# A shorter filter-band set-up, a new order of the first loads, and a later first down projection in a convolution and gated feed-forward kernel

## The chip, the cores and the metric

The kernel runs on one core of a Trainium2 chip. The metric is the device time of one execution in microseconds (us), as the median of several runs. The span in a trace, from the first to the last instruction, is about 1.8 us shorter than that time.

## The reference

```python
# x: (8, 4096, 192); weight: (8 heads, 7 taps); gate, val: (192, 1536); out: (1536, 192)
w = softmax(weight, axis=-1)
x_pad = zeros of 6 rows ahead of each sequence, then x
conv[b, s, h, :] = sum over k of w[h, k] * x_pad[b, s + k, h, :]      # 24 columns per head
y = conv.reshape(32768, 192)
g, v = y @ w_gate, y @ w_val
out = (g * sigmoid(g) * v) @ w_out
```

A causal seven-tap filter, with one set of taps per head, is followed by a gated feed-forward layer over 32,768 tokens.

## The kernel before

The convolution is a matmul with a banded matrix built from the taps, named `wide`. It is built on the chip at the start: small matmuls spread the taps over the partitions (`tapbank`), a multiplication with a unit matrix makes `spread`, and four matmuls with 0/1 matrices `shift` put the taps in their places (`taps`); two engines then copy the result out of PSUM into `wide`.

Tokens go through in 64 blocks of 512. A block has 12 steps. One step (`gate_val`) projects to 128 of the 1536 hidden columns, with six half-row matmuls that run as three pairs; ScalarE then takes the activation and VectorE the product. The down projection (`acc`) is done in four slots per block, between steps. The first four blocks have a convolution of their own (`early`), with a transpose on TensorE (`eturn`), so that the first step can start soon.

```python
    xe_load(0)                    # rows of x for block 0, three DMAs
    load_w(0, 384)                # gate and val columns, three DMAs each call
    load_w(384, 1024)
    xe_tile(1)
    xe_load(1)                    # rows of block 1
    load_w(1024, Dff)
    load_wo(0, 6)
    load_wo(6, NCH)
    # ... cut ...
    def make_wide():
        # ... cut ...
        for i in range(2):
            for n in range(2):
                matmul(banks[n], shift[:, n, i], spread[:, i],       # 512 columns
                       start=(i == 0), stop=(i == 1))
        # ... cut: two casts on ScalarE, two on VectorE into wide
    # ... cut ...
    keep_warm(7)                  # 128x512 matmuls on zeros
    spread_taps()
    keep_warm(2)
    make_wide()
    early(0, ...)
    eturn(0, ...)
    for n in range(n_steps):
        # ... cut: early(1) is the work of n == 4, early(2) of n == 10, early(3) of n == 19
        gate_val(n)
        if j % 3 == 1:
            after = silu[n - 2] if n >= 2 else None
            # j 7 and 10: slots 1 and 2 of this block; j 1 and 4: slots 3 and 4 of the last one
        # ... cut: eturn(1) after step 6, eturn(2) after step 17
```

## Time and profile before

| what | value | read from |
|---|---|---|
| time | 793.54 us, three runs of 792.71 to 794.03 | the times |
| TensorE busy | 784.0 of 792.0 us | the page |
| block 0's convolution starts | 7.57 us | timeline of TensorE |
| step 0 starts | 9.97 us | timeline of TensorE |
| step 20 starts | 34.17 us | timeline of TensorE |

Lines of the page of the kernel before: the span, the busy time of TensorE with its share and instruction count, and the granted clock in tenths over 40 slices.

```profile
span 792.0 us, 28590 instructions
...
PE 784.0 (99%) x12018; PEld 493.9 (62%) x12018; DVE 584.1 (74%) x933; ACT 522.2 (66%) x910; POOL 67.4 (9%) x93
...
PEclk9999999999999999999999999999999999999999
```

TensorE has no free time to speak of, so only the start and the end of the program can shrink. The next lines are the timeline of TensorE in the kernel before. The columns are start, length, engine, line, operation, output and inputs, the shapes and the count; an idle time before and its releaser stand in brackets.

```profile
1.20 3.17 PE L643 MATMUL warm<-fill 128*128 128x512 f16 x7 [1.20 <-DVE fill L91]
4.30 0.36 PE L286 MATMUL tapbank<-eye,split 8*32 8x8 f16 x16
4.59 1.03 PE L643 MATMUL warm<-fill 128*128 128x512 f16 x2
5.43 1.58 PE L326 MATMUL taps<-spread,shift 128*128 128x512 f16 x4
7.57 0.83 PE L380 MATMUL cv<-xe,wide 64*64 64x72 f16 x64 [0.56 <-ACT wide L338]
8.89 1.14 PE L438 MATMUL turn<-ident,tme 128*128 128x128 f16 x15 [0.50 <-ACT tme L398]
9.97 0.39 PE L545 MATMUL gate<-xc,w 64*128 64x512 f16 x1
...
13.72 0.22 PE L380 MATMUL cv<-xe,wide 64*64 64x72 f16 x1
14.50 0.72 PE L380 MATMUL cv<-xe,wide 64*64 64x48 f16 x63 [0.56 <-DMA xe<-in_x_dram]
...
30.45 0.72 PE L438 MATMUL turn<-ident,tme 128*128 128x128 f16 x10 [0.34 <-DVE o_sb L627]
```

From 5.43 to 7.57 us the chain runs through the four band matmuls and the casts. Block 1's convolution starts at 13.72 us and stops after one matmul until its rows of x land. At 30.45 us block 2's transposes wait for VectorE to take the finished output out of PSUM. Next, what the weight loads of TensorE waited for between 9 and 24 us in the kernel before: who waited, for what, the total in us, how often, the longest.

```profile
PEld L380 <- DMA xe<-in_x_dram: 0.7, 1, 0.7
...
PEld L545 <- DMA w<-in_moe_w_val_dram: 0.5, 2, 0.3
```

These are the rows of block 1 and the weights of step 3. The table by windows of the same kernel gives for each stretch the busy time of the five engines, then the clock, the mean busy share of the DMA engines, and GB/s.

```profile
4.00:6.00 2.00, 2.00 (x21) 0.84 (x21) 1.70 (x7) 0.74 (x2) 2.00 (x5) 1.00 1.25 134
6.00:8.00 2.00, 1.44 (x41) 0.60 (x42) 0.95 (x3) 0.65 (x2) 2.00 (x4) 1.00 0.99 127
```

From 4 us on the DMA engines are full. A caution about the clock column: it reads 1.00 here, while the 512-column matmuls before 7 us stand 0.43 us apart and those after 10 us stand 0.215 us apart. There is no clock record before the first grant, and the view takes full speed for granted there. The spacing of the matmuls shows the true rate.

### The profile page before, as it was taken

How to read it: one execution, taken by the hardware profiler on the slowest of the kernel's cores; microseconds unless marked ns; L12 is line 12 of the kernel's file. 1: busy time of each engine (PE TensorE's matmuls, PEld its weight loads, DVE VectorE, ACT ScalarE, POOL GpSimd, SP SyncE). 2: the span in 40 equal slices, each digit the busy share in tenths (PEclk: the TensorE clock that was granted, in tenths of full speed). 3: DMA queues.
4: the chain of work that ended last, by engine and by line, in shares of the span. 5: the costliest groups of instructions: out<-in, count | busy, mean ns of one | idle time of the engine just before them, and what ended most of it. 6: DMA issues, size and time to landing. Idle time of an engine off the chain costs nothing.

```text
span 792.0 us, 28590 instructions
## 1 busy us (share of the span) xinstructions
PE 784.0 (99%) x12018; PEld 493.9 (62%) x12018; DVE 584.1 (74%) x933; ACT 522.2 (66%) x910; POOL 67.4 (9%) x93
## 2 busy tenths in 40 slices
PE   8999999999999999999999999999999999999997
PEld 4666666666666666666666666666666666666665
DVE  7677777777777867767777777777777777777775
ACT  5676766666666666757666666666667667676664
POOL 8111010010100101001010000100001010000000
PEclk9999999999999999999999999999999999999999
DMA  9999577786857778567894769858587794726311
GB/s 131 149 204 146 125 116 118 164 124 146 105 120 152 129 147 119 120 126 125 155 140 113 117 112 165 128 133 118 112 154 121 150 115 118 136 81 116 80 42 42
DMA packets 214961, 99.23 MB, mean 125 GB/s; under 512 B 148776, under 2 KB 213936, under 8 KB 213936
## 3 DMA queue, kind: packets, MB, share of 16 engines
q1 hardware_dynamic: 167424, 78.75, 49.3%
q0 software_dynamic: 47136, 18.45, 21.7%
q8 instruction: 94, 1.54, 0.8%
q14 instruction: 35, 0.29, 0.1%
q10 hardware_dynamic: 272, 0.20, 0.1%
HBM read 36.90 MB, written 41.16 MB: 99 GB/s over the span
## 4 chain that ended last, share of the span: by engine, by line
PE 97%; DMA 1%; POOL 1%; DVE 0%; ACT 0%; issue 0%; POOLq 0%
PE gate L545 61%; PE acc L571 32%; PE cv L469 2%; PE val L545 1%; DMA xe<-in_x_dram 1%; POOL w L162 0%; POOL xe L97 0%; PE acc L592 0%; PE cv L380 0%; PE turn L438 0%; DVE h L556 0%; ACT sig L554 0%; DVE o_sb L627 0%; DVE tm L486 0%; ACT o_sb L731 0%
## 5 line engine op out<-in xcount | busy, mean ns | idle before, releaser
L556 DVE TENSOR_TENSOR h<-sig,val 128x512 f16<-128x512 f16 x768 | 507.7, 687 | 195.4 <-PE val L545 192.9
L554 ACT ACTIVATE sig<-gate 128x512 f16<-128x512 f32 x768 | 458.5, 597 | 234.9 <-PE val L545 207.4
L545 PE MATMUL val<-xc,w 64*128 64x512 f16 x2304 | 539.1, 376 | 0.2 <-DVE tm L486 0.2
L545 PE MATMUL gate<-xc,w 64*128 64x512 f16 x2304 | 539.2, 376 | 0.0
L545 PEld LDWEIGHTS <-w 64*128 64x128 f16 x4608 | 221.0, 94 | 212.7 <-issue 1.2
L571 PEld LDWEIGHTS <-h 64*128 64x128 f16 x6096 | 257.8, 94 | 66.0 <-issue 6.1
L571 PE MATMUL acc<-wo,h 64*128 64x192 f16 x6096 | 298.8, 243 | 0.0
L97 POOL DMA_DIRECT2D x<-in_x_dram x40 | 31.6, 792 | 437.0 <-ACT sig L554 429.9
L486 ACT CAST tm<-cv 128x480 f16<-128x480 f32 x60 | 30.6, 562 | 22.1 <-PE cv L469 22.1
L486 DVE CAST tm<-cv 128x480 f16<-128x480 f32 x60 | 36.6, 652 | 2.6
L627 DVE COPY o_sb<-acc 128x384 f32<-128x384 f32 x63 | 34.7, 550 | 0.0
L497 POOL COPY tm<-tm 128x1280 f16<-128x1280 f16 x15 | 18.8, 1252 | 137.3 <-DVE tm L486 129.1
L626 ACT COPY o_sb<-acc 128x384 f32<-128x384 f32 x63 | 30.1, 478 | 0.0
L469 PE MATMUL cv<-x,band 64*32 64x240 f16 x960 | 18.2, 265 | 0.0
L469 PEld LDWEIGHTS <-band 64*32 64x32 f16 x960 | 10.1, 91 | 4.9 <-issue 4.7
L132 POOL MEMSET x<- 6x192 f16 x7 | 1.7, 248 | 59.7 <-PE cv L469 59.6
L97 POOL DMA_DIRECT2D xe<-in_x_dram x9 | 6.0, 692 | 0.4 <-issue 0.3
L643 PE MATMUL warm<-fill 128*128 128x512 f16 x9 | 4.2, 628 | 1.2 <-DVE fill L91 1.2
L398 ACT CAST tme<-cv 128x288 f16<-128x288 f32 x8 | 2.9, 401 | 2.5 <-PE cv L380 2.5
L380 PE MATMUL cv<-xe,wide 64*64 64x48 f16 (+1 forms) x256 | 3.2, 192 | 1.1 <-ACT wide L338 0.6
L380 PEld LDWEIGHTS <-wide 64*64 64x64 f16 x256 | 2.7, 108 | 2.5 <-ACT wide L338 1.1
L438 PE MATMUL turn<-ident,tme 128*128 128x128 f16 x45 | 3.3, 220 | 0.8 <-ACT tme L398 0.5
(53 smaller groups left out, 40.0 us busy)
## 6 DMA issues: line engine op xcount, KB each, us to landing
out_dram<-o_sb SPq DMA_DIRECT2D x63, 384.0 KB
scr<-tm SPq DMA_DIRECT2D x105, 130.0 KB
x<-x SPq DMA_DIRECT2D x28, 480.0 KB
x<-in_x_dram POOLq DMA_DIRECT2D x24, 480.0 KB, 9.4
x<-in_x_dram POOLq DMA_DIRECT2D x7, 468.0 KB, 7.4
xc<-scr SPq DMA_TRANSPOSE x180
scr<-tm SPq DMA_DIRECT2D x15, 104.0 KB
wo<-in_moe_w_out_dram POOLq DMA_DIRECT2D x2, 288.0 KB, 6.3
```

The costliest lines, as they stand in the source:

```text
L97: nc.gpsimd.dma_start(out=t[p0 + i0 : p0 + i1, w0 - at : w1 - at, :], in_=bass.AP(tensor=x_flat.tensor, offset=(t0 + size * w0 - pad + i0) ...
L380: nc.tensor.matmul(o[Q * c : Q * c + Q, at : at + w], wide[Q * r : Q * r + Q, a, h, :], xe[e][Q * r : Q * r + Q, c : 2 * G : 2, h * grp : ...
L469: nc.tensor.matmul(banks[r][32 * c : 32 * c + 32, t * w : t * w + w], band[Q * r : Q * r + Q, h, :], x16[u][Q * r : Q * r + Q, NG * c : NG ...
L486: eng(tm[u][:, NG * r : NG * r + NG, 2 * grp * hp : 2 * grp * hp + 2 * grp].rearrange("p g (t e) -> p g t e", t=2), banks[r][:, 0 : 2 * w] ...
L497: seq(nc.gpsimd.tensor_copy(tm[u][:, :, SL * Q : 4 * Q], tm[u][:, :, 0:Q]))
L545: nc.tensor.matmul(o, w16[p0 : p0 + Q, k, ts(j, P)], xc[b][k][p0 : p0 + Q, 0:TB], start=(k == 0), stop=(k == SL - 1),)
L554: silu[n] = seq(nc.scalar.activation(sg, g, AF.Silu)).ins
L556: seq(nc.vector.tensor_tensor(hj, sg, v, op=ALU.mult))
L571: nc.tensor.matmul(acc[b][bank][:, s, :], hj[p0 : p0 + Q, ts(2 * bank + s, P)], wo16[p0 : p0 + Q, j, :], start=(not second and j == 0 and ...
L626: seq(nc.scalar.copy(o_sb[:, 0:2, :], acc[b][0]))
L627: seq(nc.vector.tensor_copy(o_sb[:, 2:4, :], acc[b][1]))
L643: nc.tensor.matmul(warm, fill[:, 0:P], fill, start=True, stop=True, skip_group_check=True,)
```

## The change

The intent is to start step 0 about a microsecond sooner and to close the holes that follow. The change has four parts. The band comes from one product of 256 columns and four half-size matmuls. The rows of x that make the first window are loaded behind the bulk. An index that is needed later is made apart, ahead of the weight loads. In block 0, the second convolution moves behind step 5 and the down projection starts at step 9.

```diff
             if e == 0 and r == 0:
-                windows(xe[e], 0, 0, EO, 0, 1, i0=pad)
                 windows(xe[e], 0, 0, EO, 1, w1)
+                windows(xe[e], 0, 0, EO, 0, 1, i0=pad, i1=Q - 2)
...
-    jid = small("jid", [P, P], i32)
-    seq(nc.gpsimd.iota(jid, pattern=[[1, P]], base=0, channel_multiplier=0))
+    jn = small("jn", [P, 4, Q], i32)
+    seq(nc.gpsimd.iota(jn, pattern=[[-16, 4], [1, Q]], base=0, channel_multiplier=0))
     xe_tile(0)
-    seq(nc.vector.memset(xe[0][0:pad, 0, :], 0.0))
+    seq(nc.vector.memset(xe[0][0:Q, 0, :], 0.0))
     xe_load(0)
+    cid = small("cid", [P, P], i32)
+    seq(nc.gpsimd.iota(cid, pattern=[[1, P]], base=0, channel_multiplier=0))
     load_w(0, 384)
...                                     # (split is widened to 16 copies of each tap)
-        for i in range(2):             # 16 tap matmuls of 8x32
-            for a in range(2):
-                for d in range(4):
+        for a in range(2):             # 2 tap matmuls of 8x128
...
-        for i in range(2):
-            for n in range(2):         # 512 columns, in pairs that accumulate
-                    nc.tensor.matmul(banks[n], shift[:, n, i], spread[:, i],
-                        start=(i == 0), stop=(i == 1))
+        for n in range(4):             # 256 columns, each its own half of a bank
+                nc.tensor.matmul(banks[n // 2][:, c0 : c0 + 256], shift[:, n], spread,
+                    start=(n % 2 == 0), stop=True)
...
     keep_warm(7)
     spread_taps()
-    keep_warm(2)
+    keep_warm(5, P)                    # five of 128 columns
     make_wide()
...
-        if n == 4:                     # work of slot 4: early(1)
-        elif n in (10, 19):            # work: early(2), early(3)
+        if n in (11, 19):              # work: early(2), early(3)
...
         gate_val(n)
+        if n == 5:
+            early(1, (*acc_banks, gate_bank))
+        elif n == 7:
+            eturn(1, (*acc_banks, gate_bank))
+        elif n in (9, 11):
+            slot(1 if n == 9 else 2, b, silu[n - 1], work)
+        elif n == 13:
+            slot(3, 0, silu[n - 1])
+        elif j % 3 == 1 and b:         # as before
...
+        if n == 18:                    # was 17
             eturn(2, (*acc_banks, gate_bank))
```

More of the change, by code (lines that the diff above doesn't have):

```diff
@@ L202 @@
             load_x(1, r, low=low)
-    pm_i = small("pm_i", [P, 1], i32)
-    seq(nc.vector.tensor_single_scalar(pm_i, pid, 31, op=ALU.bitwise_and))
-    pm = small("pm", [P, 1])
-    seq(nc.vector.tensor_copy(pm, pm_i))
-    jf = small("jf", [P, P])
-    seq(nc.vector.tensor_copy(jf, jid))
-    p32 = small("p32", [P, 1])
-    seq(nc.vector.tensor_tensor(p32, pid, pm, op=ALU.subtract))
-    pd = small("pd", [P, 1])
-    eye = small("eye", [P, 32], fp16)
+    pq_i = small("pq_i", [P, 1], i32)
+    seq(nc.vector.tensor_single_scalar(pq_i, pid, 15, op=ALU.bitwise_and))
@@ L214 @@
+    pq = small("pq", [P, 1])
+    seq(nc.vector.tensor_copy(pq, pq_i))
+    pk = small("pk", [P, 1])
+    seq(nc.vector.tensor_tensor(pk, pid, pq, op=ALU.subtract))
+    eye = small("eye", [P, 16], fp16)
     seq(
         nc.vector.tensor_scalar(
-            eye, jf[:, 0:32], scalar1=pm, scalar2=None, op0=ALU.is_equal
+            eye, jn[:, 0, 0:16], scalar1=pq, scalar2=None, op0=ALU.is_equal
         )
     )
-    seq(
-        nc.vector.tensor_scalar(pd, p32, scalar1=1.0 / 32, scalar2=None, op0=ALU.mult)
-    )
@@ L222 @@
-    both = small("both", [P, 1])
-    seq(nc.vector.tensor_tensor(both, pm, pd, op=ALU.add))
-    eyes = small("eyes", [P, 32, 2, H], fp16)
-    seq(
-        nc.scalar.copy(
-            eyes.rearrange("p j a h -> p j (a h)"),
-            eye.unsqueeze(2).to_broadcast([P, 32, 2 * H]),
-        )
-    )
-    shift = small("shift", [P, 2, 2, 2, Q], fp16)
-    def make_shift(n, i):
-        seq(
-            nc.vector.tensor_scalar(
-                shift[:, n, i],
-                jf[:, 0:Q].unsqueeze(1).to_broadcast([P, 2, Q]),
-                scalar1=both, scalar2=32.0 * n + 4.0 * i,
-                op0=ALU.subtract, op1=ALU.is_equal,
-            )
-        )
@@ L243 @@
-    wexp = small("wexp", [H, K + 1])
-    seq(nc.vector.memset(wexp[:, K : K + 1], 1e-9))
-    split = small("split", [H, 2, K + 1], fp16)
-    seq(nc.vector.memset(split, 0.0))
-    make_shift(0, 0)
-    make_shift(1, 0)
+    eyes = small("eyes", [P, 16, 2 * H], fp16)
+    seq(nc.scalar.copy(eyes, eye.unsqueeze(2).to_broadcast([P, 16, 2 * H])))
+    both = small("both", [P, 1])
+    seq(
+        nc.vector.scalar_tensor_tensor(
+            both, pk, 1.0 / 16, pq, op0=ALU.mult, op1=ALU.add
+        )
+    )
@@ new lines, with make_shift @@
+    wexp = small("wexp", [H, K + 1])
+    seq(nc.vector.memset(wexp[:, K : K + 1], 1e-9))
+    split = small("split", [H, 2, K + 1, 16], fp16)
+    seq(nc.vector.memset(split[:, :, K, :], 0.0))
+    shift = small("shift", [P, 4, 2, Q], fp16)
+    def make_shift(n):
+        seq(
+            nc.vector.tensor_tensor(
+                shift[:, n : n + 2],
+                jn[:, n : n + 2].unsqueeze(2).to_broadcast([P, 2, 2, Q]),
+                both.unsqueeze(2).unsqueeze(3).to_broadcast([P, 2, 2, Q]),
+                op=ALU.is_equal,
+            )
+        )
@@ L250 @@
+    make_shift(0)
     wmax = small("wmax", [H, 1])
@@ L254 @@
     seq(nc.scalar.activation(warmed, fill[:, 0:1], AF.Silu))
-    make_shift(0, 1)
+    make_shift(2)
     wsum = small("wsum", [H, 1])
@@ L258 @@
     seq(nc.vector.reciprocal(wsum, wsum))
+    wide_exp = wexp[:, 0:K].unsqueeze(2).to_broadcast([H, K, 16])
     seq(
-        nc.vector.tensor_scalar(
-            split[:, 0, 0:K], wexp[:, 0:K], scalar1=wsum, scalar2=None, op0=ALU.mult
+        nc.vector.tensor_tensor(
+            split[:, 0, 0:K],
+            wide_exp,
+            wsum.unsqueeze(2).to_broadcast([H, K, 16]),
+            op=ALU.mult,
         )
@@ L266 @@
             split[:, 1, 0:K],
-            wexp[:, 0:K],
+            wide_exp,
             wsum,
@@ L273 @@
     )
-    make_shift(1, 1)
-    tap = small("tap", [P, 2, 2, H], fp16)
-    spread = small("spread", [P, 2, 32, 2, H], fp16)
+    tap = small("tap", [P, 2 * H], fp16)
+    spread = small("spread", [P, 16, 2, H], fp16)
     def spread_taps():
         bank = apool.tile([P, TB], fp32, tag="acc0", name="tapbank")
-        for i in range(2):
-            for a in range(2):
-                c0 = (2 * i + a) * H
-                for d in range(4):
-                    k = 4 * i + d
-                    seq(
-                        nc.tensor.matmul(
-                            bank[32 * d : 32 * d + 32, c0 : c0 + H],
-                            split[:, a, k : k + 1].to_broadcast([H, 32]),
-                            eye[0:H, 0:H],
-                            start=(c0 == 0),
-                            stop=True,
-                            skip_group_check=True,
-                            tile_position=(0, 32 * d),
-                        )
-                    )
-        seq(
-            nc.vector.tensor_copy(
-                tap.rearrange("p i a h -> p (i a h)"), bank[:, 0 : 4 * H]
-            )
-        )
-        for i in range(2):
-            seq(
-                nc.vector.tensor_tensor(
-                    spread[:, i].rearrange("p j a h -> p j (a h)"),
-                    eyes.rearrange("p j a h -> p j (a h)"),
-                    tap[:, i]
-                    .rearrange("p a h -> p (a h)")
-                    .unsqueeze(1)
-                    .to_broadcast([P, 32, 2 * H]),
-                    op=ALU.mult,
-                )
-            )
+        for a in range(2):
+            seq(
+                nc.tensor.matmul(
+                    bank[:, a * H : a * H + H],
+                    split[:, a].rearrange("h k q -> h (k q)"),
+                    eye[0:H, 0:H],
+                    start=(a == 0),
+                    stop=True,
+                    skip_group_check=True,
+                )
+            )
+        seq(nc.vector.tensor_copy(tap, bank[:, 0 : 2 * H]))
+        seq(
+            nc.vector.tensor_tensor(
+                spread.rearrange("p j a h -> p j (a h)"),
+                eyes,
+                tap.unsqueeze(1).to_broadcast([P, 16, 2 * H]),
+                op=ALU.mult,
+            )
+        )
     wide = small("wide", [P, 2, H, Q], fp16)
@@ L322, in make_wide @@
         ]
-        for i in range(2):
-            for n in range(2):
-                seq(
-                    nc.tensor.matmul(
-                        banks[n],
-                        shift[:, n, i].rearrange("p r i -> p (r i)"),
-                        spread[:, i].rearrange("p j a h -> p (j a h)"),
-                        start=(i == 0),
-                        stop=(i == 1),
-                    )
+        for n in range(4):
+            c0 = 16 * 2 * H * (n % 2)
+            seq(
+                nc.tensor.matmul(
+                    banks[n // 2][:, c0 : c0 + 16 * 2 * H],
+                    shift[:, n].rearrange("p r i -> p (r i)"),
+                    spread.rearrange("p j a h -> p (j a h)"),
+                    start=(n % 2 == 0),
+                    stop=True,
+                    skip_group_check=True,
                 )
+            )
         seq(nc.vector.tensor_copy(pf, pid))
@@ L346, in make_wide @@
             nc.vector.tensor_scalar(
-                ident, jf, scalar1=pf, scalar2=None, op0=ALU.is_equal
+                ident, cid, scalar1=pf, scalar2=None, op0=ALU.is_equal
             )
@@ L638, with keep_warm @@
     warm = ppool.tile([P, TB], fp32, tag="gate", name="warm")
-    def keep_warm(count):
+    def keep_warm(count, width=TB):
         for _ in range(count):
@@ L643, in keep_warm @@
                 nc.tensor.matmul(
-                    warm, fill[:, 0:P], fill, start=True, stop=True,
-                    skip_group_check=True,
+                    warm[:, 0:width], fill[:, 0:P], fill[:, 0:width],
+                    start=True, stop=True, skip_group_check=True,
                 )
@@ L663, with work @@
         work = None
-        if n == 4:
-            def work():
-                early(1, (*acc_banks, gate_bank))
-        elif n in (10, 19):
-            def work(e=2 if n == 10 else 3):
+        if n in (11, 19):
+            def work(e=2 if n == 11 else 3):
                 early(e, (gate_bank, gate_bank, val_bank))
@@ L679 @@
         gate_val(n)
-        if j % 3 == 1:
-            after = silu[n - 2] if n >= 2 else None
-            if j == 1:
-                if b:
-                    slot(3, b - 1, after)
-            elif j == 4:
-                if b:
-                    slot(4, b - 1, after)
-                if work:
-                    work()
-            else:
-                slot(1 if j == 7 else 2, b, after, work)
-        if u == 0:
-            if ls == 6:
-                eturn(1, (*acc_banks, gate_bank))
-            if ls == 17:
-                eturn(2, (*acc_banks, gate_bank))
-            if ls == 20:
-                eout(3)
-            if ls == 21:
-                efetch(3)
+        if n == 5:
[7 more added lines that the diff above has]
+        elif j % 3 == 1 and b:
+            k = {1: 3, 4: 4, 7: 1, 10: 2}[j]
+            slot(k, b - 1 if j < 7 else b, silu[n - 2], work if j > 4 else None)
+            if j == 4 and work:
+                work()
+        if n == 18:
+            eturn(2, (*acc_banks, gate_bank))
+        elif n == 20:
+            eout(3)
+        elif n == 21:
+            efetch(3)
         if u + 1 < NU:
```

## The prediction

> **What bounds the kernel now.** TensorE. The page gives it 784.0 us busy of 792.0; the chain of waits is 97% TensorE; the clock row is 9 throughout. The timeline shows a projection step (three pairs of half-row matmuls) every 0.645 us and twelve pairs of down matmuls in 0.99 us, back to back after 36 us. The change touches none of that. It can win only in the first 36 us: the first projection is issued at 9.97 us, and short holes follow.
>
> **Holes after 10 us (TensorE timeline and waits):** 0.15 us between the first two pairs; 0.3 at step 3, for the second slice of gate and value weights (landing 12.2 and 12.6); 0.8 at 13.6-14.5, where block 1's convolution waits for its rows of x (landing 14.5); 0.1 at the transposes at 16.5; 0.15 in the first down slot; 0.4 at 30, where block 2's transposes wait for the output eviction. About 1.9 in all.
>
> **Band.** Now: 16 tap matmuls 0.36 us, tap copy 0.19, two spreads of 0.38, four 512-column matmuls 0.43 apart (5.43-7.0), wide casts to 7.8, convolution at 7.57. The skill's page "TensorE: Matmul & The Clock Gate", section "Wait — 56ns, not 53.3ns?", gives 427 ns cold and 216 warm for 512 columns; this trace agrees (0.43 before 7 us, 0.215 after 10). After: two tap matmuls, one 256-column spread, four 256-column matmuls each finishing half a bank. Estimate: 0.85 less on matmuls, 0.15-0.2 less on the spread, 0.1 more for wider splits. Taps can't start before about 4.3, since seven warm-up matmuls (3.0 us) stand ahead. Step 0 starts about 1 us earlier, near 9.0.
>
> **Why most of that is lost.** From 4 us the DMA engines are saturated (DMA share over 1, 110-145 GB/s). Step 3's weights and block 1's rows arrive when the stream delivers them; the band gain becomes a longer wait. The stream moves little: bulk rows issued first start full flow about 0.5 us earlier, but the first-window rows (22 KB) join the stream, the 256-column index costs 0.1 more on GpSimd, and the column index 0.2 before the weight issues. Estimate: landings 0.1-0.4 earlier; I take 0.25.
>
> **Schedule.** Block 1's convolution after step 5, not 4, puts one step (0.645 us) into the wait for its rows; 0.2-0.5 of wait remains. Down at steps 9, 11, 13 waits for the activation of the step just before, which ends about 0.2 after the current step's last issue (timeline: activation starts 0.4 after a step's last pair, lasts 0.6). Cost 0.2 each, 0.45 net of the present slot-1 hole. Block 2's transposes one step later save 0.35.
>
> **Sum:** 0.25 (stream) + 0.65 (step in the wait) + 0.35 + 0.1 (small holes) - 0.45 = 0.9 us. Everything later shifts by this. Predicted 792.6 us, 80% range 791.6 to 793.4. Chances: over 2% faster 0.01, within 2% 0.985, over 2% slower 0.005.
>
> **What would show it.** Band matmuls 0.21 us apart; first convolution at 6.4-6.8; first projection at 8.8-9.2; a weight wait of 1.0-1.3 us at step 3; block 1's convolution after six steps, ending 14.7-15.1; small holes before the slots at 9, 11, 13; none at block 2's transposes; the steady part unchanged.
>
> **What would make it wrong.** Loads landing 0.5 us or more earlier (gain 1.2-1.6); the array not at full clock when step 0 starts, since the shorter band leaves it idle more (loss up to 1 us); VectorE falling behind in ten steps without down (0.66 against 0.645 us a step); wider holes at the three slots.

## The result, and the profile after

The changed kernel took 793.55 us (median of four runs, 792.81 to 794.03), and the kernel before 793.78 us in its four runs (792.71 to 794.28). The ratio is 0.9998 with a 95% interval of 0.9981 to 1.0015. Ratios here are the mean time of one kernel's runs over that of the other's of the same rounds, so they are not quite the ratio of the medians. "Within 2%" was forecast. The 792.6 us was not, and 793.55 lies outside the stated range of 791.6 to 793.4.

The page of the kernel after, the same lines as above:

```profile
span 791.0 us, 28566 instructions
...
PE 783.5 (99%) x12007; PEld 493.2 (62%) x12007; DVE 583.2 (74%) x928; ACT 522.1 (66%) x910; POOL 67.7 (9%) x94
...
PEclk9999999999999999999999999999999999999999
```

The timeline of TensorE after, and of its weight loads (PEld) for the slot lines:

```profile
4.30 0.21 PE L279 MATMUL tapbank<-eye,split 8*128 8x8 f16 x2
4.44 0.71 PE L628 MATMUL warm<-fill 128*128 128x128 f16 x5
5.10 0.99 PE L310 MATMUL taps<-spread,shift 128*128 128x256 f16 x4
6.66 0.83 PE L365 MATMUL cv<-xe,wide 64*64 64x72 f16 x64 [0.56 <-ACT wide L323]
7.98 1.05 PE L423 MATMUL turn<-ident,tme 128*128 128x128 f16 x15 [0.50 <-ACT tme L383]
8.98 0.37 PE L530 MATMUL gate<-xc,w 64*128 64x512 f16 x1
...
13.48 0.22 PE L365 MATMUL cv<-xe,wide 64*64 64x72 f16 x1
13.85 0.72 PE L365 MATMUL cv<-xe,wide 64*64 64x48 f16 x63 [0.15 <-DMA xe<-in_x_dram]
...
18.35 0.94 PEld L556 LDWEIGHTS <-h 64*128 64x128 f16 x24 [0.53 <-ACT sig L539]
...
29.44 1.01 PE L423 MATMUL turn<-ident,tme 128*128 128x128 f16 x15
```

What the weight loads waited for between 9 and 24 us in the kernel after:

```profile
PEld L556 <- ACT sig L539: 1.1, 2, 0.5
PEld L530 <- DMA w<-in_moe_w_val_dram: 0.7, 2, 0.4
...
PEld L365 <- DMA xe<-in_x_dram: 0.3, 1, 0.3
```

Most marks of the prediction are there. The band matmuls are 0.2 us apart, the convolution starts at 6.66 us, step 0 at 8.98 us, one more step is done before block 1's convolution, the slots wait for the activation, and block 2's transposes no longer wait. One mark is missing: the weight wait at step 3 was forecast at 1.0 to 1.3 us, and the weight loads waited 0.7 us, since the last of these weights landed at 11.79 us and not at 12.58 as before. Step 20 starts at 33.00 us in place of 34.17, so this execution was 1.17 us ahead. From the start of step 20 to the last projection the two traces take the same 750.64 us to within 5 ns, and so do ten of the other twelve traces below. The question is therefore not where the gain went within this execution. Its span is 1.0 us shorter, and its time was 792.81 us. It was the fastest of its four runs, however, and the median of the four shows a quarter of that gain.

### The profile page after: what moved, and what is told of

It is laid out like the page before. It is cut to its first block, busy times and chain, and to the rows that moved or that the text cites. A ratio compares the mean times of both kernels' runs of the same rounds, so it can differ in the third digit from the quotient of the medians.

```text
span 791.0 us, 28566 instructions
## 1 busy us (share of the span) xinstructions
PE 783.5 (99%) x12007; PEld 493.2 (62%) x12007; DVE 583.2 (74%) x928; ACT 522.1 (66%) x910; POOL 67.7 (9%) x94
## 4 chain that ended last, share of the span: by engine, by line
PE 97%; POOL 1%; DMA 1%; DVE 0%; ACT 0%; issue 0%; POOLq 0%
PE gate L530 61%; PE acc L556 32%; PE cv L454 2%; PE val L530 1%; DMA xe<-in_x_dram 1%; POOL w L162 0%; POOL xe L97 0%; PE acc L577 0%; PE cv L365 0%; PE turn L423 0%; DVE h L541 0%; ACT sig L539 0%; DVE tm L471 0%; ACT o_sb L710 0%; DVE o_sb L612 0%
## 5 line engine op out<-in xcount | busy, mean ns | idle before, releaser
L628 PE MATMUL warm<-fill 128*128 128x512 f16 (+1 forms) x12 | 3.9, 494 | 1.2 <-DVE fill L91 1.2
L365 PE MATMUL cv<-xe,wide 64*64 64x72 f16 (+1 forms) x256 | 3.2, 192 | 0.7 <-ACT wide L323 0.6
L162 POOL DMA_DIRECT2D w<-in_moe_w_val_dram x6 | 3.6, 623 | 0.0
```

The lines of the kernel that those rows point to most:

```text
L365: nc.tensor.matmul(o[Q * c : Q * c + Q, at : at + w], wide[Q * r : Q * r + Q, a, h, :], xe[e][Q * r : Q * r + Q, c : 2 * G : 2, h * grp : ...
L628: nc.tensor.matmul(warm[:, 0:width], fill[:, 0:P], fill[:, 0:width], start=True, stop=True, skip_group_check=True,)
```

## The experiments

All twelve kernels gave correct results. Each was timed in five rounds; kernels of one set share a chip and the runs of the kernel before. Landing times are the issue of a DMA plus its time to landing in the trace. The moments at which full clock was granted come from the clock records in the trace, and the spacing of the matmuls agrees with them.

### First set: the change again, and its parts

The unchanged text of the changed kernel, run again:

> The changed kernel again, to size the difference. The two traces agree to the nanosecond from step 20 on and differ by 1.16 us there, yet four runs each gave medians only 0.23 us apart. Theory A (the gain is real, about 1.0 us, and single runs scatter by over 1 us because the array's full clock is granted at another moment in each run): the mean of ten or so runs is 0.7 to 1.2 us below before, and runs with a mean clock of 0.999 are the longer ones in both kernels. Theory B (the profiled run was a lucky one; in most runs the shorter warm-up makes the clock come later and takes the gain back): the mean is within 0.3 us of before, and the changed kernel has more runs at clock 0.999 than before has.

The new band and load order with the old schedule of block 0 (the edit in short, not line by line):

```diff
-        if n == 5: early(1) ... slots at 9, 11, 13 ... eturn(2) at 18
+        # the loop head of the kernel before: early(1) in n == 4, slots from 7, eturn(2) at 17
```

> New band and new load order, old schedule of block 0 (block 1's convolution inside step 4, down from step 7). My theory that the loads decide: step 3 waits for weights to about 11.4 to 11.8 as in the changed kernel, block 1's convolution waits from about 12.9 to 13.85, one step fewer in the wait; the gain at step 20 is only the earlier landing, about 0.65 us, with the hole at block 2's transposes back. Rival (the chain through the band decides): it keeps most of the 1.0 us by which step 0 is earlier, 0.95 to 1.1 us.

The old band and load order with the new schedule, which is the same swap the other way round:

> Old band and old load order, new schedule of block 0. Loads land as before (weights of step 3 at 12.2 and 12.6, block 1's rows at 14.5), so one more step fits into the wait, plus 0.35 to 0.4 us at block 2's transposes, minus 0.2 us at each of the slots of steps 11 and 13: gain at step 20 of 0.5 to 0.7 us. If the slots cost more than I think, it is 0.2 us or less.

The changed kernel with the old order of the first two loads:

```diff
-                windows(xe[e], 0, 0, EO, 1, w1)
-                windows(xe[e], 0, 0, EO, 0, 1, i0=pad, i1=Q - 2)
+                windows(xe[e], 0, 0, EO, 0, 1, i0=pad)
+                windows(xe[e], 0, 0, EO, 1, w1)
...
-    seq(nc.vector.memset(xe[0][0:Q, 0, :], 0.0))
+    seq(nc.vector.memset(xe[0][0:pad, 0, :], 0.0))
```

> The changed kernel with the first window's rows again ahead of the bulk. My prediction gave the load order 0.25 us; the trace has step 3's weights and block 1's rows landing 0.65 to 0.8 us earlier. If the order is what did that, the landings go back to about 12.2, 12.6 and 14.5 and 0.6 to 0.8 us of the gain at step 20 is lost. If something else moved them (the index work on GpSimd, less sharing with VectorE), they stay within 0.2 us of 11.4, 11.8 and 13.85.

| kernel | five runs, us | median | ratio to before |
|---|---|---|---|
| changed | 793.25, 795.12, 793.80, 793.37, 793.43 | 793.43 | 1.0001 |
| band and order only | 794.60, 793.32, 793.76, 793.32, 793.62 | 793.62 | 0.9997 |
| schedule only | 793.73, 793.28, 793.01, 793.33, 793.48 | 793.33 | 0.9995 |
| order undone | 795.21, 793.39, 793.37, 793.25, 793.77 | 793.39 | 1.0001 |
| before (nine runs) | 793.63 to 793.90 | 793.76 | |

Every interval includes 1. Theory A expected 0.7 to 1.2 us, and it is wrong: the changed kernel's typical run is 0.3 us below before. Theory B has the better of it: the mean of the five is within 0.1 us of before. But its "in most runs" is not what happened; one run in five is 1.7 us longer than the rest. The mean clock of the runs does not sort them as expected. The 795.12 us run has clock 1.000 and the 793.37 us run 0.998. As said above, that figure does not see the start.

The traced run of "order undone" was itself the long one, and it shows the cause. Full clock was granted at 13.63 us, against 5.94 and 6.40 us in the two traces of the changed kernel so far. Steps 0, 1 and 2 started 1.25 us or more apart, and step 20 started at 35.31 us. The traced run of "band and order only" (794.60 us) is another thing. Its clock came at 5.67 us and its step 20 started at 33.89 us, but it lost 0.90 us in two stops later in the program. There the profile names no releaser, so those stops are left unexplained. Up to step 20 this trace answers its own question. Step 0 started at 8.96 us, as early as in the changed kernel, and then the convolution of block 1 waited for its rows, the last of which landed at 14.18 us:

```profile
PEld L365 <- DMA xe<-in_x_dram: 1.1, 1, 1.1
```

Step 20 was 0.28 us ahead of the first trace of before and 0.15 us behind the second one (told below). The rival's 0.95 to 1.1 us is out; the 0.65 us of the theory was not reached either. The schedule alone missed its forecast in the trace as well: step 20 at 33.96 us is 0.20 us ahead of the first trace of before, where 0.5 to 0.7 was expected, with block 1's rows landing at 14.77 us.

Undoing the order cost nothing in the times: without the long run in each, four runs have means of 793.45 and 793.46 us. In that trace step 3's last weights land at 12.69 us and block 1's last rows at 14.01 us. The repeated changed kernel has 12.22 and 14.23, and its first trace 11.79 and 13.81. So the same kernel's loads scatter by 0.4 us between these two runs (by 1.0 us with its third trace below, where the rows land at 13.27 us), and one pair of traces says little about an order.

### Second set: is it the clock, and do the loads gate?

The changed kernel with the holes of TensorE filled:

```diff
...                                     # keep_warm is given the tile that it writes
     make_wide()
+    keep_warm(6, P)
     early(0, (gate_bank, gate_bank, val_bank))
+    warm2 = ppool.tile([P, TB], fp32, tag="val", name="warm2")
+    keep_warm(6, P, warm2)
     eturn(0, (*acc_banks, gate_bank))
```

> The changed kernel with six 128-column warm-up matmuls before block 0's convolution and six between it and the transposes, so that TensorE has no hole between its first instruction and step 0. The clock theory (in some runs the windows over which the array's activity is judged fall so that the hole at 6.1 to 6.7 us denies full clock, and steps 0 to 2 then run at half speed, as in the profiled run of 795.21 us with full clock only from 13.6 us): no run over 794.0, full clock from 8 us at the latest in the profile, mean 0.2 to 0.5 us below the changed kernel's, median 793.1 to 793.5. If the outliers have another cause, such as loads landing late or a stray hiccup, they stay at about one run in five.

The changed kernel beside it:

> The changed kernel once more, in the same rounds as the filled one. Clock theory: four of five runs at 793.2 to 793.8, about one at 794.5 to 795.3. If the first outlier was a stray hiccup: none.

The changed kernel with hardly any warm-up:

```diff
-    keep_warm(7)
+    keep_warm(1)
     spread_taps()
-    keep_warm(5, P)
```

> The changed kernel with one warm-up matmul in place of twelve, to size a late clock: every run should get full clock only at 10 to 14 us, with steps 0 to 2 at 1.25 us each until then. If a late clock costs what the outlier shows, the median is 794.3 to 795.3, that is 0.9 to 1.9 us above the changed kernel, and the spread is wide. If the waits for loads absorb it, it is within 0.3 us of the changed kernel, and the outliers need another cause.

The second weight load cut in two:

```diff
-    load_w(384, 1024)
+    load_w(384, 640)
+    load_w(640, 1024)
```

> The changed kernel with the second weight load cut in two (columns 384 to 640, then 640 to 1024), so that step 3's weights land about 1 us sooner. If both loads gate in turn, the wait at step 3 shrinks to under 0.3 us, but block 1's convolution then waits that much longer for its rows, which still land at about 14.2, and the time stays within 0.2 us of the changed kernel. If step 3's weights alone hold back the band's gain, 0.4 us or more comes back.

| kernel | five runs, us | median | ratio to before |
|---|---|---|---|
| filled | 793.33, 792.88, 793.46, 794.26, 793.43 | 793.43 | 0.9997 |
| changed | 795.22, 793.46, 793.95, 793.78, 793.01 | 793.78 | 1.0002 |
| hardly any warm-up | 795.49, 794.56, 794.72, 794.73, 794.85 | 794.73 | 1.0012 |
| weight load cut in two | 793.70, 794.96, 793.30, 794.91, 793.80 | 793.80 | 1.0005 |
| before (nine runs) | 793.15 to 794.18 | 793.70 | |

This time the long run of the changed kernel is the traced one. The timeline of TensorE in that run:

```profile
5.11 1.01 PE L310 MATMUL taps<-spread,shift 128*128 128x256 f16 x4
6.69 1.17 PE L365 MATMUL cv<-xe,wide 64*64 64x72 f16 x64 [0.56 <-ACT wide L323]
8.35 1.78 PE L423 MATMUL turn<-ident,tme 128*128 128x128 f16 x15 [0.49 <-ACT tme L383]
10.06 0.60 PE L530 MATMUL gate<-xc,w 64*128 64x512 f16 x1
...
10.46 0.63 PE L530 MATMUL gate<-xc,w 64*128 64x512 f16 x1
...
10.89 0.63 PE L530 MATMUL gate<-xc,w 64*128 64x512 f16 x1
```

And the filled kernel, the same view:

```profile
5.11 1.01 PE L310 MATMUL taps<-spread,shift 128*128 128x256 f16 x4
5.91 0.84 PE L628 MATMUL warm<-fill 128*128 128x128 f16 x6
6.69 0.82 PE L365 MATMUL cv<-xe,wide 64*64 64x72 f16 x64
7.44 0.51 PE L628 MATMUL warm<-fill 128*128 128x128 f16 x6
8.01 1.04 PE L423 MATMUL turn<-ident,tme 128*128 128x128 f16 x15
9.01 0.37 PE L530 MATMUL gate<-xc,w 64*128 64x512 f16 x1
...
9.45 0.37 PE L530 MATMUL gate<-xc,w 64*128 64x512 f16 x1
...
9.66 0.37 PE L530 MATMUL gate<-xc,w 64*128 64x512 f16 x1
```

In the long run the same convolution takes 1.17 us in place of 0.82, the transposes 1.78 in place of 1.04, and pairs of a step are 0.42 us apart in place of 0.215. Full clock came at 14.02 us there and at 6.78 us in the filled run. The filled kernel's forecast held in its trace and its mean (0.41 us below the changed kernel's), but not in "no run over 794.0": one run took 794.26 us. The Trainium skill ("TensorE: Matmul & The Clock Gate", "What's actually happening") says that activity is judged over windows of 3413 ns that run freely, whatever the kernel does. The clock records agree: full clock lasts 785.065 us in most traces, which is 230 such windows, and 778.239 us, or 228, in the run with order undone and in this long run. A grant that is missed came two windows later in both late traces of this start.

Two traces nearly share a window. With the order undone, the window of 3.39 to 6.80 us (worked out as the last 3.41 us before 6.80, two windows ahead of the grant) holds the hole of 0.56 us ahead of the convolution, and no grant followed. The lines of that run:

```profile
6.68 1.17 PE L365 MATMUL cv<-xe,wide 64*64 64x72 f16 x64 [0.56 <-ACT wide L323]
8.34 1.78 PE L423 MATMUL turn<-ident,tme 128*128 128x128 f16 x15 [0.49 <-ACT tme L383]
```

In the filled kernel the window of 3.37 to 6.78 us has no such hole, and full clock was granted at its end. This is one pair of traces, but it is the comparison that the theory asked for. The window after the missed one, to 10.22 us, holds the second hole, of 0.49 us, which may be why two windows were lost and not one. A part of the hole does not deny the grant: the repeated changed kernel got full clock at 6.40 us, 0.3 us into the same hole.

The kernel with hardly any warm-up was to show the price where every run is a candidate. Its median is 0.95 us above the changed kernel's of the same rounds, at the low end of the forecast, and its spread is not wide: four of five runs lie within 0.3 us. Its traced run (795.49 us) got full clock at 11.92 us, but it is a poor witness: it lost 0.9 us between steps 11 and 12 and 0.57 us after step 20 in stops for which the profile names no releaser, and block 1's rows landed at 14.90 us, the latest of all traces. So the 0.95 us is known from the times, and how much of it is the clock is not shown.

The cut weight load moved the wait, as the two-gate theory says. In its trace, the weight loads waited between 9 and 24 us for:

```profile
PEld L366 <- DMA xe<-in_x_dram: 1.7, 1, 1.7
PEld L557 <- ACT sig L540: 1.1, 2, 0.5
...
PEld L531 <- DMA w<-in_moe_w_val_dram: 0.4, 1, 0.4
```

Step 3 no longer waits (it runs from 10.61 to 11.33 us, 0.72 us, where the step in the filled trace took 1.27). Block 1's convolution waits 1.7 us instead, for rows that land at 14.79 us. The rows were not left alone, though: the cut adds three DMA issues ahead of them, so the last one was issued at 9.50 us and not at 7.77, and 14.2 us was forecast. Step 0 started at 8.45 us in this run, since full clock happened to come at 3.97 us, and even so step 20 started only at 33.99 us. Step 20 came 19.195 us after the rows; half a microsecond more at the front did not bring it forward.

### Third set: the noise, the repaired version, and another load order

The kernel before against itself:

> The kernel before against itself, for the noise of the comparison and a second profile of it. Expected: ratio 1.000 with an interval of about 0.001 each way, no run more than 0.8 us above the median, full clock by 8 us at the latest. If the first profile of before was typical, block 1's rows land at 14.2 to 14.7; if loads simply scatter from run to run as they did in the eight other profiles (13.3 to 14.9), anywhere in there.

The filled kernel again:

> The filled version of the changed kernel again. Clock theory: again no run above 794.3, mean 0.2 to 0.4 us below before. If its first five runs were only lucky, one or two of five come out at 794.5 to 795.3.

The schedule alone again:

> Old band and load order with the new schedule, again. Clock theory: the old band keeps the array busy to 7.0 us and has no late clock, so no run above 794.2, mean 0.3 to 0.4 us below before, that is as good as the filled version with the new band; the band's 1 us then is worth nothing by itself. Rival: the earlier band is worth something once the clock is early, and the filled version is 0.2 us or more below this one.

The filled kernel with loads in the order of need and a schedule to suit:

```diff
-    load_w(384, 1024)
+    load_w(384, 640)
     xe_tile(1)
     xe_load(1)
+    load_w(640, 768)
+    load_w(768, 1024)
     load_w(1024, Dff)
...
...                                     # and the fillers as above; the schedule in short:
-    early(1) after step 5, eturn(1) after 7, slots at 9, 11, 13
+    early(1) after step 4, eturn(1) after 6, slots at 10, 12, 14; slot 4 at 16 waits for silu[n - 1]
```

> The filled version with the loads in the order in which they are needed: weight columns 384 to 640, block 1's rows, 640 to 768, 768 to 1024, the rest; block 1's convolution after step 4, its transposes after step 6, down at steps 10, 12, 14. If the loads are what holds the start back, step 3 no longer waits, block 1's convolution starts right after step 4 at about 12.4, and step 8 starts 0.5 to 1.0 us earlier than in the filled version: median 792.4 to 793.0. If the total of the stream or the weights of the down projection (landing 17.5 to 18.4) hold it back instead, the gain moves into a wait at step 5, at step 8 or at the first down slot, and the time is within 0.2 us of the filled version.

| kernel | five runs, us | median | ratio to before |
|---|---|---|---|
| before, against itself | 793.52, 793.71, 793.36, 793.60, 793.95 | 793.60 | 0.9997 |
| filled | 793.01, 793.06, 793.72, 792.85, 793.10 | 793.06 | 0.9991 |
| schedule only | 793.42, 793.24, 793.61, 793.08, 792.77 | 793.24 | 0.9992 |
| loads in order of need | 793.66, 793.54, 795.83, 794.24, 794.20 | 794.20 | 1.0007 |
| before (nine runs) | 793.39 to 794.99 | 793.71 | |

The kernel before came out at 0.9997 of itself, with full clock at 6.39 us in its trace. Its second trace matters more than its ratio. Here is what its weight loads waited for between 9 and 24 us:

```profile
PEld L545 <- DMA w<-in_moe_w_val_dram: 0.8, 2, 0.5
...
PEld L380 <- DMA xe<-in_x_dram: 0.2, 1, 0.2
```

In the first trace of the same kernel the wait for block 1's rows was 0.7 us; here it is 0.2 us, since the rows landed at 14.02 us and not at 14.46. Step 20 started at 33.73 us and not at 34.17. The prediction's largest term was sized on that wait.

The filled kernel and the schedule alone, each with five runs and none over 793.8 us, have means of 793.15 and 793.22 us: as good as each other, as the clock theory forecast, and both more below before (793.83) than the 0.2 to 0.4 us expected.

The kernel with loads in order of need failed, and by more than its rival expectation said: that one had the time within 0.2 us of the filled version, and the median is 1.1 us above it. Step 3 did not wait and block 1's convolution ran at 12.74 us at once, but the wait moved to the next weights:

```profile
PEld L532 <- DMA w<-in_moe_w_val_dram: 1.5, 2, 0.9
PEld L558 <- ACT sig L541: 0.8, 2, 0.5
```

The last weights landed at 17.84 us and the first half of the down weights at 19.96 us, against 15.65 and 17.23 in the filled kernel. The two extra load calls add six DMA issues of about 0.6 us each on GpSimd, so the weights behind them are issued later. Its run of 795.83 us has no trace, and its cause is open.

## Why the prediction was right or wrong

**The mechanism up to step 20 was right.** The front gained 1.0 us as forecast (8.98 against 9.97), the three slots cost 0.2 us each (the last pair at 17.94 should have been followed at 18.15 and the slot began at 18.35), and block 2's transposes lost their wait. That the loads swallow the front's gain can be read from seven traces in which block 1's convolution waited for its rows. Step 20 starts 19.71 us after the landing of these rows under the old schedule (both traces of before, band and order only) and 19.19 to 19.20 us after it under the new one (the two traces of the changed kernel with early clock, the first of the schedule alone, the cut weight load). Step 0 started anywhere from 8.45 to 9.97 us in these seven, and it made no difference. The 0.52 us between the two schedules is the step in the wait, 0.645 us, less 0.13 us of net slot cost, where the prediction had the slots and the small holes at zero (0.35 + 0.1 - 0.45).

**The step that failed is the sum, at its two terms that loads decide: "0.25 (stream)" and "0.65 (step in the wait)".** Both were sized on one trace of before, as if the landings in it were constants. They are not. Over all fourteen traces step 3's last weights landed between 11.79 and 12.89 us where their load was not cut, and block 1's last rows between 13.27 and 14.90 where the load order was not altered.

- The stream: in the first pair of traces the rows landed 0.65 us earlier than before, so step 20 came 0.65 + 0.52 = 1.17 us earlier, where 0.9 was forecast. Between the second trace of before (14.02) and the repeated changed kernel (14.23) they landed 0.21 us later, and step 20 came only 0.31 us earlier.
- The step in the wait: the prediction wrote "puts one step (0.645 us) into the wait for its rows; 0.2-0.5 of wait remains". In the two early-clock traces of the changed kernel 0.3 us remained, as forecast. But the second trace of the schedule alone and both filled traces show no wait for rows at all, and then a part of the step is lost. After step 3 gets its weights, block 1's convolution can start about 1.0 us later under the old schedule and 1.65 us later under the new one. It starts at the later of that moment and the landing of the rows. With the landings of the second trace of before (weights 12.75, rows 14.02) one more step would end at 14.40, and 0.38 of the 0.645 us would be lost. Done in this way for the twelve traces whose weight load was not cut, the mean loss is 0.17 us, an estimate from those landings.

Which of the two terms fell short in the runs without a trace stays open. With the stream at zero, as the order experiment's times suggest, the estimate at step 20 is 0.645 - 0.17 - 0.13 = 0.35 us. The two traces of each kernel with early clock show twice that, 33.00 and 33.42 us against 34.17 and 33.73, but the changed kernel's two (792.81 and 793.25 us) were the fastest runs of their sets.

**A cost at the end was not foreseen.** From the last projection to the end of the program, the kernel before takes 7.24 and 7.28 us in its two traces, and the changed kernel 7.40 to 7.41 in its three. In the traces of before and of the changed kernel the difference comes after the final clearing of semaphores on GpSimd: the clearing takes 0.14 us in both, but the DRAIN instruction behind it ends 7.16 to 7.18 us after the last projection and not 6.72 to 6.76. It is not settled what sets it: the kernel with the cut weight load, which has the new band too, took 7.30 us. Taking 0.14 us from 0.35 leaves 0.21 us. The changed kernel's twelve runs of normal length have a mean of 793.50 us against 793.71 us of before in the same rounds, a difference of 0.21 us. The agreement is an estimate that fits, not a measurement of its terms.

**The load order's 0.25 us cannot be shown.** In the seven traces with the new order and uncut weights the rows landed on average 0.4 us sooner than in the five with the old one (13.96 against 14.34), but single traces of one kernel differ by more, and undoing the order left the times as they were. The forecast of 0.1 to 0.4 us is neither confirmed nor refuted.

**A risk was named and then priced at zero.** The prediction listed "the array not at full clock when step 0 starts, since the shorter band leaves it idle more (loss up to 1 us)", and neither the sum nor the range held anything for it. Two of the changed kernel's fourteen runs were about 1.7 us longer than the rest, and the traced one of them shows this cause. The mean of all fourteen is 793.74 us against 793.71 us of before, so this takes the rest of the gain. The other long run has no trace. Over all rounds, among kernels with the new band and open holes 6 of 29 runs were over 794.5 us (three were traced: two show the late clock, one does not). With the old band it was 1 of 46, untraced, and with the holes filled 0 of 10, or 1 of 15 with the other load order. At a rate of 6 in 29, ten runs without a long one come by chance about once in ten times (an estimate), so the counts set the new band with open holes apart from the old band, but they do not prove that filling the holes repairs it. The band's shortening took away matmuls that had kept the array busy up to 7.0 us, and moved the hole forward to 6.1. What share of a window has to be busy is not settled: the trace with the cut weight load got full clock at 3.97 us, although TensorE's first matmul began only at 1.20 us.

**The base was a noisy median.** The 792.6 us was counted from 793.54 us, a median of three runs; 31 runs of before in these rounds have means of 793.64 to 793.83 us per set. The 80% range of 1.8 us was about as wide as the scatter of single runs, but it was centred on a gain that only the best runs showed.

**What each part is worth.** The schedule alone (ten runs, mean 793.30 us) is 0.5 us faster than before in its rounds (793.79), and the filled version with everything (ten runs, 793.31 us against 793.76 us) is no faster than that. The shorter band therefore shows no worth in these times, with or without the fillers. The likely reasons are the wait of step 3 and block 1 for loads and the 0.14 us at the end. The traces do not exclude a small gain: the filled kernel's step 20 came at 33.47 and 33.18 us, that of the schedule alone at 33.96 and 33.73, although the latter two runs (793.73 and 793.42 us) were slower than that kernel's mean. Both versions have lower means than before in each set they ran in, and than the changed kernel in the sets where it ran beside them. The differences are under 0.1%, and the intervals against before include 1, so this is a likely but small improvement.

## What to carry to other kernels

Shortening a set-up chain pays only up to the next gate, so look first at what arrives when; where a stream of loads feeds the start, time saved ahead of it comes out again as a wait on a DMA. A wait read from one trace of a start that depends on loads is one draw: take two or three traces before sizing a term of half a microsecond on it, and give a risk that you can name a probability and a cost in the sum. Idle matmuls that look useless may be what brings the clock up in time; when they or the work around them are cut, check the spacing of matmuls in several runs, not the average clock.

## What the Trainium skill lacked or had wrong

- "TensorE: Matmul & The Clock Gate", "What's actually happening": the window of 3413 ns agrees with the runs (785.065 us is 230 of them). "What you observe" puts the scatter of the transition at 500 ns each way; in the kernels with full warm-up here it came at 3.97 to 6.78 us in eleven traces, that is 2.8 to 5.6 us after the first matmul at 1.20, and at 13.63 and 14.02 us in two, two windows late. No section gives the share of a window that must be busy, which the late traces here leave open.
- No page says that the granted clock in a profile is blind before its first record: a run of 795.21 us with half speed up to 13.6 us shows a mean clock of 0.999, and one of 793.37 us shows 0.998.
- "DMA: Bandwidth & Descriptors", "Anatomy of one DMA — SWDGE (gpsimd) path", gives about 2.0 us fixed; the first load here took 2.1 us (1.42 to 3.56) and agrees. It has nothing on scatter: behind a full stream the same rows landed at 13.27 to 14.90 us in different runs.
- No page says what makes the end of a program vary: from the last projection on, programs with the same work there took 6.98 to 7.48 us; between before and the changed kernel (7.24 and 7.40) the difference comes after the final semaphore clearing on GpSimd.
